# An adaLN block on one core: the attention gate spread by TensorE, one x load on another queue, and a new written-out order

## The chip, the cores and the metric

The kernel runs on one core of a Trainium2 chip. The metric is the device time in microseconds (us) of one execution, given as the median over several executions; lower is better. The core's engines are named as the profile names them: PE (TensorE, with PEld for its weight loads), DVE (VectorE), ACT (ScalarE), POOL (GpSimd) and SP (SyncE, which only issues DMAs here). A q behind a name (SPq, ACTq) stands for an engine's instruction queue when it issues DMAs.

## The reference

x has 2048 rows of 640 values, in bf16. A condition vector c gives six rows of 640, `mod = silu(c) @ w_mod`: shift, scale and gate for the attention (sa, ca, ga) and for the feed-forward part (sb, cb, gb).

```python
h = layernorm(x) * (1 + ca) + sa
x = x + ga * attention(h)      # 32 heads of 20, window of 256 keys, causal
h = layernorm(x) * (1 + cb) + sb
x = x + gb * ((sigmoid(h @ w_gate) * (h @ w_up)) @ w_down)   # 1536 wide
```

Attention is `softmax(q k^T / sqrt(20)) v @ wo`, where a row sees itself and the 255 rows before it.

## The kernel before, in words

The rows are worked in eight chunks of 256 (two blocks of 128). For each chunk the kernel does: statistics and normalisation (DVE and POOL), a transposition of the normalised rows to hT, scaling and shifting, the projection to q, k and v (PE, `proj`), transposition of q and k, attention in two halves of 16 heads, the output projection (`wo`), the second normalisation, and the feed-forward part (`mlpg`, `mlpu`, `down`). Transpositions of chunks 0 to 2 are matmuls against an identity (`aptr`, `qtr`), later ones are DMA transposes on SP's queue (`atr`, `qkt`, `btr`).

A half of attention is five score sets on PE (chunk 0 has three), each followed by its exponentials on ACT (line 1015). All score sets write the one PSUM tile S, so a score set waits for the exponentials of the one before. POOL then masks the exponentials (line 1040). The product with v of one half (`pv`, line 669 with E and V) is issued together with the second score set of the next half, except in chunk 0, where it stands alone. All other products of PE go to four PSUM buffers, the pool M. A `pv` needs two neighbouring buffers of it.

The gates are worked into weights: row-wise products make `wo` into `wo * ga` (line 1253, `wos`, five DVE instructions) and `w_down` into `w_down * gb` (line 1192, `wds`). For that each of the 128 partitions needs the whole gate. `mod_rows` computes it: 20 small matmuls (`modb`) leave the row in four 160-wide strips on four groups of 32 partitions, one DVE instruction (line 710, `gq`) copies the strips to SBUF, and then there are two ways, chosen by the tuple `GB`. With the index in `GB`, TensorE spreads the row (`spread` and `evg`). Otherwise the row goes through DRAM: one small DMA writes it (line 731, `gate`), another reads it back to all partitions (`gatebc`). Both gates use the one buffer `gq` and the one buffer `gbc`. In the kernel before `GB` is empty.

The other half of the PSUM tile of `modb` holds a shift or scale row. It is transposed by DVE (line 736, `modt`) through the tile T1, which attention's normalisation (line 1082) uses too, and the M buffer is held until then.

The order of all 2121 operations is written out. The n-th entry of the list `PRIO` belongs to the n-th operation that the program creates. Its remainder by 5 is the engine (0 PE, 1 ACT, 2 DVE, 3 POOL, 4 SP), and the operations of an engine run in rising order of the entries. A planner in the kernel only picks buffers by estimated times; the waits on the chip come from the data and from buffers that are reused.

At the start ACT's queue issues the load of c, and SP's queue issues x block 0, the first fifth of the scale and shift columns of w_mod (`wm0`, five slices of 320 KB into the space of `wd`), x block 1, the other four slices, then pieces of wqkv. Matmuls without use warm PE meanwhile. The shift and scale (`modA`, tile S, ten matmuls for each slice) end in `mA` (line 761), which hT of chunk 0 needs (lines 846 and 847).

Of the kernel before, what the change touches and what calls it, by code (L numbers as in the profile page):

```python
# [336 lines left out]
def c_pe(n):  # L337
# [5 lines left out]
    23, 28, 258, 8, 43, 33, 958, 18, 1448, 38, 3, 507, 513, 72, 67, 48, 53, 58, 76, 84, 104, 99, 144, 149, 154, 159,  # L343
    164, 344, 169, 334, 329, 174, 584, 734, 739, 754, 604, 759, 749, 764, 594, 120, 177, 181, 192, 197, 62, 105,
    110, 115, 130, 135, 13, 125, 200, 205, 210, 215, 220, 225, 230, 345, 370, 352, 599, 2054, 1659, 1649, 729, 744,
    92, 87, 187, 237, 242, 247, 253, 263, 272, 267, 280, 275, 290, 300, 305, 286, 317, 296, 322, 311, 376, 357, 386,
    367, 362, 412, 422, 391, 417, 396, 380, 400, 406, 620, 655, 672, 515, 521, 820, 827, 465, 470, 476, 530, 535,
    541, 495, 501, 665, 677, 480, 485, 491, 565, 570, 576, 545, 551, 630, 652, 525, 555, 561, 625, 660, 681, 685,
    691, 930, 977, 765, 770, 792, 915, 920, 927, 805, 810, 816, 830, 835, 841, 437, 432, 442, 427, 447, 452, 458,
    463, 642, 647, 890, 845, 775, 900, 710, 897, 852, 797, 907, 787, 980, 985, 996, 1150, 1165, 1171, 1095, 1101,  # L350
    1375, 1382, 1195, 1250, 1257, 1262, 1210, 1296, 1385, 1392, 990, 1105, 1111, 1080, 1085, 1092, 1365, 1371, 1300,
    1351, 940, 945, 951, 971, 1155, 1161, 1190, 1231, 1215, 1220, 1226, 1280, 1285, 1292, 1330, 1337, 1344, 1619,
    1347, 1502, 2249, 1434, 2959, 1669, 1622, 1917, 1932, 2107, 2137, 1395, 1497, 1664, 2754, 1627, 1847, 339, 589,
    1022, 637, 1037, 802, 782, 912, 1043, 1048, 1053, 1058, 1237, 1485, 1410, 1455, 1435, 1305, 1492, 1421, 1462,
    1442, 1317, 1570, 1575, 1581, 1515, 1520, 1527, 1844, 1585, 1590, 1632, 1751, 1839, 1905, 1965, 2041, 2020,
    2030, 2037, 2059, 2070, 2080, 2086, 2142, 2094, 1820, 1830, 1922, 1970, 2075, 2152, 719, 724, 1007, 1002, 1017,
    1012, 937, 1027, 1033, 1063, 1068, 1203, 1242, 1209, 1249, 1453, 1548, 1536, 1543, 1471, 605, 611, 616, 695,
    706, 701, 855, 961, 881, 871, 861, 968, 888, 878, 868, 1115, 1127, 1122, 1137, 1142, 1147, 1736, 1716, 1726,
    1416, 1941, 1070, 1076, 1131, 1175, 1181, 1186, 1265, 1321, 1401, 1356, 1271, 1328, 1408, 1363, 1278, 1505,
    1597, 1512, 1602, 1612, 1772, 1896, 1891, 1886, 1881, 2046, 2310, 2315, 2322, 2155, 2160, 2327, 2205, 2210,  # L360
    2227, 2395, 2400, 2432, 2337, 2332, 2507, 2437, 2502, 2512, 2518, 2523, 2527, 2537, 2534, 2544, 2717, 2756,
    2777, 2772, 2767, 2739, 2734, 2969, 3074, 3022, 3312, 3327, 3027, 3032, 3037, 3317, 3502, 3507, 3322, 3413,
    3418, 2865, 2870, 2875, 2890, 2895, 2760, 2845, 2880, 2885, 2905, 2901, 2912, 3045, 3050, 3075, 3080, 3085,
    2915, 2920, 3055, 3060, 3065, 3091, 3097, 3110, 3115, 3170, 3175, 3180, 3100, 3105, 3185, 3195, 3200, 3191,
    3232, 3205, 3210, 3215, 3220, 3225, 3240, 3245, 3250, 3265, 3270, 3236, 3277, 3280, 3285, 3290, 3295, 3330,
    3300, 3375, 3380, 3385, 3390, 3336, 3422, 3430, 3435, 3445, 3450, 3470, 3440, 3575, 3580, 3585, 3590, 3476,
    3597, 3640, 3645, 3655, 3727, 3650, 3730, 3780, 3817, 3859, 3740, 3745, 3750, 3827, 3900, 3905, 3910, 3917,
    4476, 1700, 1705, 1862, 1710, 1800, 1902, 1914, 1690, 1695, 1746, 1782, 2189, 2390, 2405, 2412, 2145, 2300,
    2307, 2429, 2250, 2260, 2267, 2616, 2749, 1865, 1875, 1937, 1825, 1975, 1992, 1429, 1314, 1607, 1637, 1787,
    1767, 1777, 1792, 1798, 1853, 2008, 2178, 1963, 2128, 2184, 2134, 2367, 2371, 2386, 2381, 2376, 1465, 1481,  # L370
    1476, 1530, 1556, 1566, 1670, 1731, 1676, 1721, 1741, 1805, 1816, 1811, 1870, 1946, 2001, 2025, 2061, 2066,
    1553, 1763, 1758, 1563, 1688, 1683, 1928, 1858, 1953, 1958, 2013, 2018, 2095, 2101, 2231, 2202, 2217, 2222,
    2592, 2597, 2984, 2964, 2999, 2989, 3129, 2255, 2286, 2271, 2341, 2281, 2345, 2351, 2356, 2440, 2456, 2451,
    2465, 2485, 2496, 2460, 2580, 2587, 3399, 2695, 2700, 2817, 2951, 3409, 2620, 2625, 2631, 2445, 2490, 2562,
    3404, 2665, 2670, 2787, 2792, 4199, 2640, 2655, 2662, 2705, 2710, 2841, 1654, 1644, 1997, 1987, 2122, 1982,
    2112, 2117, 2168, 2173, 2193, 2243, 2603, 2608, 2424, 2744, 3346, 3261, 3306, 3041, 3011, 2565, 2576, 2571,
    2238, 2298, 2293, 2198, 2473, 2278, 2363, 2483, 2478, 2548, 2553, 2558, 2635, 2676, 2686, 2652, 2647, 2782,
    2812, 2822, 2974, 2994, 2979, 3004, 3124, 3545, 3550, 3557, 3455, 3540, 3562, 3530, 3535, 3677, 3610, 3615,
    3682, 3572, 3567, 3672, 3687, 3692, 3697, 3703, 3708, 3867, 3712, 3929, 3719, 4213, 4208, 4081, 4132, 4232,
    4220, 4280, 4285, 4290, 4325, 4215, 4310, 4315, 4320, 4335, 4331, 4357, 4345, 4350, 4370, 4375, 4380, 4340,  # L380
    4390, 4395, 4400, 4405, 4386, 4412, 4420, 4425, 4430, 4435, 4440, 4415, 4540, 4545, 4550, 4555, 4511, 4582,
    4560, 4565, 4570, 4585, 4605, 4590, 4595, 4610, 4615, 4620, 4696, 4702, 4705, 4710, 4715, 4725, 4755, 4720,
    4730, 4735, 4800, 4805, 4761, 4812, 4815, 4820, 4825, 4830, 4840, 4835, 4845, 4855, 4860, 4865, 4851, 4872,
    4900, 4905, 4910, 4917, 5215, 5220, 5225, 5382, 5389, 5175, 5180, 5185, 5192, 5360, 5365, 5400, 5407, 5934,
    2690, 2831, 2801, 2826, 2796, 2850, 2856, 2861, 2925, 3016, 3006, 3135, 3141, 3146, 2613, 2838, 2948, 2683,
    2933, 2808, 2938, 3158, 2943, 3133, 3168, 3163, 3350, 3371, 3366, 3357, 3362, 3427, 3512, 3842, 3864, 3849,
    3874, 3854, 4494, 3460, 3486, 3481, 3466, 3491, 3605, 3621, 3631, 3660, 3761, 3666, 3735, 3890, 3896, 4180,
    4185, 4247, 5034, 4105, 4115, 4122, 4177, 5164, 4110, 4160, 4167, 3885, 3970, 4047, 4174, 3995, 4000, 4006,
    4097, 5029, 3980, 3985, 3991, 4135, 4140, 4242, 2724, 2419, 3722, 2727, 3822, 3497, 3807, 3877, 3883, 3948,
    4067, 4052, 4194, 4204, 4793, 4896, 5061, 4978, 5066, 3765, 3771, 3776, 3153, 3523, 3798, 3528, 3518, 3603,  # L390
    3628, 3803, 3638, 3788, 3758, 3793, 3920, 3931, 3936, 3977, 4102, 4127, 4462, 4467, 4484, 4499, 4474, 4489,
    4649, 4920, 4930, 4987, 4925, 4940, 4992, 5015, 5020, 5077, 4935, 5050, 5082, 5002, 4997, 5007, 5092, 5087,
    5097, 5103, 5108, 5122, 5132, 5154, 5159, 5346, 5351, 5323, 5356, 5328, 5475, 5495, 5530, 5535, 5540, 5455,
    5510, 5515, 5520, 5525, 5546, 5567, 5570, 5575, 5580, 5585, 5590, 5550, 5555, 5560, 5600, 5605, 5596, 5612,
    5670, 5675, 5750, 5780, 5785, 5775, 5830, 5835, 5855, 5870, 5891, 5902, 5885, 5905, 5910, 6005, 6010, 5875,
    5880, 5915, 5920, 5925, 6016, 6022, 6050, 6055, 6060, 6065, 6070, 6025, 6030, 6035, 6040, 6045, 6076, 6082,
    6105, 6110, 6115, 6120, 6125, 6130, 6135, 6140, 6145, 6150, 6156, 6172, 6325, 6330, 6335, 6342, 6760, 6820,
    6860, 6867, 6871, 6670, 6775, 6780, 6787, 6825, 6960, 6965, 6972, 6979, 4020, 4031, 4026, 4036, 4041, 4145,
    4151, 4156, 4250, 4256, 4271, 4360, 4446, 4366, 3943, 4298, 4093, 4013, 4238, 4088, 4228, 4268, 4263, 4278,
    4308, 4303, 4450, 4531, 4526, 4517, 4502, 4522, 4627, 4632, 5044, 4659, 4654, 4639, 5059, 4600, 4661, 4686,  # L400
    4681, 4666, 4740, 4746, 4766, 4875, 4881, 4886, 6455, 6485, 6492, 6480, 6520, 6527, 6539, 6500, 6505, 6551,
    6556, 6564, 6515, 6580, 6587, 6375, 6380, 6497, 6594, 6595, 6600, 6606, 6616, 6614, 5230, 5235, 5377, 5410,
    5480, 5486, 3259, 3341, 3957, 3952, 3962, 3812, 3832, 3837, 3968, 4018, 4057, 4062, 4079, 4074, 4783, 4578,
    4772, 4507, 4692, 4960, 4971, 4966, 4458, 4673, 4678, 4538, 4788, 4778, 4753, 4958, 4798, 4948, 4893, 4953,
# [60 lines left out]
KEEP = 3  # L465
# [841 lines left out]
```

## Time and profile before

| | |
|---|---|
| median of 3 runs | 327.32 us (327.22 to 328.8) |
| profiled execution | 326.59 us |
| its span, first to last instruction | 324.9 us |
| PE busy | 316.7 us (97%) |
| DVE, ACT, POOL busy | 211.9, 212.0, 186.5 us |
| granted PE clock | 1.000 |

The span is what the profile's views are measured on; 1.69 us of the execution's time lie around it. Busy times of an engine are the time in which at least one of its instructions is in flight. A timeline row gives the start, the time that the merged group takes, the engine, the line, the operation, output and input tiles with their shape, the count, and in brackets the idle time of the engine before it and what ended that.

### The profile page before, as it was taken

How to read it: one execution, taken by the hardware profiler on the slowest of the kernel's cores; microseconds unless marked ns; L12 is line 12 of the kernel's file. 1: busy time of each engine (PE TensorE's matmuls, PEld its weight loads, DVE VectorE, ACT ScalarE, POOL GpSimd, SP SyncE). 2: the span in 40 equal slices, each digit the busy share in tenths (PEclk: the TensorE clock that was granted, in tenths of full speed). 3: DMA queues.
4: the chain of work that ended last, by engine and by line, in shares of the span. 5: the costliest groups of instructions: out<-in, count | busy, mean ns of one | idle time of the engine just before them, and what ended most of it. 6: DMA issues, size and time to landing. Idle time of an engine off the chain costs nothing.

```text
span 324.9 us, 11597 instructions
## 1 busy us (share of the span) xinstructions
PE 316.7 (97%) x4872; PEld 222.4 (68%) x4873; DVE 211.9 (65%) x424; ACT 212.0 (65%) x316; POOL 186.5 (57%) x276
## 2 busy tenths in 40 slices
PE   6999999989999999999999999999999999999997
PEld 2565544546876568765786467877786788787885
DVE  5687998778688859674477475837463769264332
ACT  1798986788966687787687867786767764011120
POOL 5119769986658694847585939382939681013000
PEclk9999999999999999999999999999999999999999
DMA  7999599989891373824304483340214032202101
GB/s 232 371 306 337 151 259 202 144 174 215 255 159 22 80 107 81 151 57 105 84 23 80 99 115 95 91 71 5 81 40 88 3 78 53 77 20 64 40 2 40
DMA packets 71694, 37.85 MB, mean 117 GB/s; under 512 B 45274, under 2 KB 70362, under 8 KB 71642
## 3 DMA queue, kind: packets, MB, share of 16 engines
q1 hardware_dynamic: 69088, 35.14, 46.3%
q10 hardware_dynamic: 2554, 1.97, 2.4%
q8 instruction: 38, 0.62, 0.7%
q14 instruction: 14, 0.11, 0.1%
HBM read 21.30 MB, written 5.25 MB: 82 GB/s over the span
## 4 chain that ended last, share of the span: by engine, by line
PE 92%; ACT 3%; DMA 2%; issue 1%; SPq 1%; ACTq 0%; DVE 0%
PE M L668 76%; PE S L669 8%; PE M L669 7%; ACT E L1015 2%; DMA wd<-in_w_mod_dram 2%; SPq L570 1%; ACT hT L811 0%; ACTq L570 0%; ACT hT L839 0%; DVE hT L858 0%; ACT hT L846 0%; PE S L668 0%; DVE x L1230 0%
## 5 line engine op out<-in xcount | busy, mean ns | idle before, releaser
L1015 ACT ACTIVATE E<-S 128x512 bf16<-128x512 f32 (+2 forms) x184 | 150.9, 879 | 48.0 <-PE S L669 47.2
L1040 POOL TENSOR_SCALAR_AFFINE_SELECT E<-E 128x512 bf16<-128x512 bf16 (+1 forms) x176 | 141.9, 832 | 69.1 <-ACT E L1015 67.4
L668 PE MATMUL M<-wqkv,hT 128*128 128x480 bf16 (+1 forms) x340 | 74.0, 355 | 0.6 <-ACT hT L846 0.5
L668 PE MATMUL M<-h2T,wu 128*128 128x256 bf16 x480 | 68.1, 273 | 0.0
L668 PE MATMUL M<-h2T,wg 128*128 128x256 bf16 x480 | 67.8, 273 | 0.0
L668 PE MATMUL M<-wd,hh 128*128 128x320 bf16 (+2 forms) x396 | 58.1, 296 | 0.0
L1211 DVE SCALAR_TENSOR_TENSOR hh<-sig,M 128x512 bf16<-128x512 f32 x48 | 32.5, 681 | 38.1 <-ACT sig L1209 25.6
L1209 ACT ACTIVATE sig<-M 128x512 f32<-128x512 f32 x48 | 28.8, 603 | 43.6 <-PE M L668 41.5
L668 PEld LDWEIGHTS M<-h2T,wu 128*128 128x128 bf16 x480 | 45.9, 98 | 7.7 <-issue 0.4
L668 PEld LDWEIGHTS M<-h2T,wg 128*128 128x128 bf16 x480 | 45.6, 98 | 7.2
L668 PEld LDWEIGHTS M<-wqkv,hT 128*128 128x128 bf16 x340 | 30.1, 98 | 27.6 <-DMA wqkv<-in_A_wqkv_dram 1.7
L668 PEld LDWEIGHTS M<-wd,hh 128*128 128x128 bf16 x396 | 36.8, 98 | 14.3 <-DVE hh L1211 0.2
L669 PEld LDWEIGHTS S<-QT,KT 20*64 20x64 bf16 (+1 forms) x1856 | 19.9, 100 | 21.2 <-ACT E L1015 12.0
L1230 DVE TENSOR_TENSOR x<-M,x 128x320 bf16<-128x320 f32 (+2 forms) x33 | 15.6, 476 | 27.2 <-PE M L668 27.1
L669 PE MATMUL S<-QT,KT 20*64 20x256 bf16 (+5 forms) x1856 | 32.1, 228 | 1.1 <-ACT E L1015 1.1
L776 DVE BATCH_NORM_STATS2 st<-x 128x6 f32<-128x320 bf16 x64 | 28.6, 477 | 2.2 <-DMA x<-in_A_x_dram 1.8
L1082 DVE STREAM_TRANSPOSE T<-M 128x512 f32<-128x512 f32 x32 | 21.5, 697 | 9.5 <-PE S L669 8.3
L668 PE MATMUL M<-wo,oT 128*128 128x320 bf16 x160 | 25.4, 300 | 0.0
L669 PE MATMUL M<-E,V 128*32 128x128 bf16 (+1 forms) x960 | 22.8, 246 | 1.0 <-ACT E L1015 0.4
L781 POOL TENSOR_SCALAR st<-st 128x2 f32<-128x2 f32 x16 | 3.7, 233 | 34.8 <-DVE st L778 34.6
L669 PEld LDWEIGHTS M<-E,V 128*32 128x32 bf16 x960 | 19.2, 97 | 5.5 <-issue 3.1
L1091 DVE STREAM_TRANSPOSE On<-Tn 128x1024 bf16<-128x1024 bf16 x16 | 19.8, 1240 | 0.3
(77 smaller groups left out, 238.9 us busy)
## 6 DMA issues: line engine op xcount, KB each, us to landing
x<-in_A_x_dram SPq DMA_DIRECT2D x24, 160.0 KB, 3.4
doc<-On SPq DMA_DIRECT2D x56, 40.0 KB
wd<-in_B_w_down_dram SPq DMA_DIRECT2D x4, 480.0 KB
wd<-in_w_mod_dram SPq DMA_DIRECT2D x5, 320.0 KB
wqkv<-in_A_wqkv_dram SPq DMA_DIRECT2D x4, 400.0 KB
wu<-in_w_mod_dram SPq DMA_DIRECT2D x5, 320.0 KB
out_dram<-x SPq DMA_DIRECT2D x9, 160.0 KB
oT<-doc SPq DMA_DIRECT2D x7, 192.0 KB, 2.8
```

What stands on the lines that cost most here:

```text
L570: return e.dma_start(dst(), src())
L668: return e.matmul(o, l, r, start=st, stop=sp, skip_group_check=True)
L669: return e.matmul(o, l, r, start=st, stop=sp, tile_position=tp, skip_group_check=True)
L776: A("dve", lambda e, g, bi=bi, j=j: e.bn_stats(v(bi * 12 + j * 6, 6), src[bi].ap[:, j * 320:(j + 1) * 320]), 0.48, reads=[src[bi].r()], wr ...
L781: A("pool", lambda e, g: e.tensor_scalar(v(28, n), var(), EPS, None, op0=ALU.add), 0.2, reads=[st.r(("m", bi)) for bi in range(n)], writes ...
L1015: A("act", lambda e, eng: e.activation(dst(), src(), ACT.Exp, scale=SM_SCALE), c_act(n), reads=[Sp.r()], writes=[E.r(key)], prio=3, tag=f" ...
L1040: A("pool", lambda e, eng: e.affine_select(rows(dst), rows(src), pattern=[[0, 8], [sign, n]], compare_op=ALU.is_ge, fill=0.0, base=base, c ...
L1082: A("dve", lambda e, g, h=h: e.transpose(T1.ap[:, 512 * h:512 * h + 512], X[h].ap), 0.694, reads=[X[h].r()], writes=[T1.r(h)], prio=3.5, t ...
L1091: A("dve", lambda e, g: e.transpose(On.ap[:], Tn.ap[:]), 1.22, reads=[Tn.r()], writes=[On.r()], prio=4, tag=f"tr2_{a}")
L1209: A("act", lambda e, g, pg=pg, sg=sg: e.activation(sg.ap[:], pg.ap[:], ACT.Tanh, scale=0.5), c_act(512), reads=[pg.r()], writes=[sg.r()], ...
L1211: A("dve", lambda e, g, pu=pu, sg=sg, f0=f0: e.scalar_tensor_tensor(out=hh.ap[:, f0:f0 + 2, :], in0=sg.ap[:].rearrange("p (a b) -> p a b", ...
L1230: A("dve", lambda e, g, ps=ps, bi=bi, c0=c0, n=n: e.tensor_tensor(x1[bi].ap[:, c0:c0 + n], ps.ap[:, 0:n], x1[bi].ap[:, c0:c0 + n], op=ALU. ...
```

## The change

Four edits, with the list replaced by one of 2123 entries:

```diff
-GB = ()
+GB = (1,)
...
     def load_x(pool, b, prio, tmin=0.0, eng="sp", extra=()):
...
-            tag=f"x{b}" ..., eng=eng, lat=0.6 if b < 2 else 0.2 + DSAFE, extra=extra)
+            tag=f"x{b}" ..., eng=eng, lat=(0.6, 0.9)[b] if b < 2 else 0.2 + DSAFE, extra=extra)
...
-    keep[0], keep[1] = load_x(p_x1, 0, 0), load_x(p_x1, 1, 0, tmin=1.2)
+    keep[0], keep[1] = load_x(p_x1, 0, 0), load_x(p_x1, 1, 0, eng="act", tmin=1.25)
```

`tmin` and `lat` are figures for the planner alone. With `GB = (1,)` the first of the two `mod_rows`, the attention's gate, takes the branch that was there unused. For each half of the row two matmuls with a broadcast column of the identity as weights copy a strip to all partitions (`gbm`), and one instruction moves 128x320 values from PSUM to `gbc` (`gbe`):

```python
for half in range(2):
    pb = Tile(p_M, "gb")
    def spread(e, g, half=half, pb=pb):
        for j in (2 * half, 2 * half + 1):
            ins = mm(e, pb.ap[:, j % 2 * 160:j % 2 * 160 + 160], ident[:, 32 * j:32 * j + 1].to_broadcast([128, 128]), gq[:],
                     j % 2 == 0, True)
        return ins
    ...
    def evg(e, g, half=half, pb=pb):
        ...
        return e.activation(dst, src, ACT.Copy) if g == "act" else e.tensor_copy(dst, src)
```

The feed-forward gate still goes through DRAM. The new list puts the first `gbe` on DVE and the second on ACT. Read out by engine around the gate, the two lists give (operation and its running number; hyphen: before, plus: after):

```diff
 PE
-aptr2#4 modb#0 qtr1#4 qtr1#1 qtr1#3 modb#1 aptr2#1 aptr2#3 aptr2#2 score1#0 aptr2#0 pvs0#1 projq2#2 projq2#3 score1#1 projq2#0 projq2#1 projk2#0 projk2#1 score1#2
+aptr2#4 qtr1#5 modb#0 qtr1#4 aptr2#1 aptr2#3 gbm#0 qtr1#1 qtr1#3 score1#0 modb#1 aptr2#2 gbm#1 aptr2#0 pvs0#1 projq2#2 score1#1 projq2#3 projk2#0 projq2#0 projq2#1 score1#2
 DVE
-ahTe2#4 gq#0 modt#0 evqt1#1 evqt1#3 ahTe2#3 ahTe2#2 ahTe2#0 gq#1 modt#1 tr1_0#3 evqk2#1 tr1_0#2
+ahTe2#4 evqt1#5 gq#0 modt#0 ahTe2#3 gbe#0 evqt1#1 evqt1#3 ahTe2#2 gq#1 wos#0 modt#1 amodu3#3 tr1_0#3 astats4#0 tr1_0#2
 ACT
-exp0#13 n_ow_0#3 ahTe2#1 amodu3#4 exp1#1 exp1#0 amodu3#2 exp1#2
+exp0#13 ahTe2#1 exp1#1 gbe#1 ahTe2#0 exp1#0 n_ow_0#3 amodu3#1 exp1#2
 SP, start
-x0 wm0#0 x1 wm0#1 wm0#2 wm0#3 wm0#4 wq wk x3 x2 wk x4 wq wv x5
+x0 wm0#0 wm0#1 wm0#2 wm0#3 wm0#4 wk wq x2 x3 wk wq x5 x4 wv
 SP, feed-forward gate
-btr0 btr0 x12 wd wd atr5 qkt3 gatebc#1 wu1
+btr0 btr0 wd gate#1 x13 wu1 wd gatebc#1 atr5 qkt3
```

`ahTe2` moves a transposed block of chunk 2 from PSUM to hT with scale and shift, `tr1_0` reads the product `pvs0` out of PSUM, `evq..` are moves out of PSUM. Elsewhere some 75 operations change their engine between ACT, DVE and POOL or their place by a few; among them four of the five scalings of h2T of chunk 0 (`bmodu0`) go from DVE to POOL. Up to the score sets and products of attention that close each stage, PE has the same operations to do in both lists, but for a few that cross such a mark and for the two new `gbm`.

More of the change, by code (lines that the diff above doesn't have):

```diff
@@ L597, in load_x @@
         dma(lambda: t.ap[:], lambda: x_flat[b * 128:(b + 1) * 128, :], 0.5, writes=[t.r()], prio=prio, tmin=tmin,
-            tag=f"x{b}" if pool is p_x0 or b < 2 * KEEP else f"y{b}", eng=eng, lat=0.6 if b < 2 else 0.2 + DSAFE, extra=extra)
+            tag=f"x{b}" if pool is p_x0 or b < 2 * KEEP else f"y{b}", eng=eng, lat=(0.6, 0.9)[b] if b < 2 else 0.2 + DSAFE, extra=extra)
         return t
```

234 rows, old and new, of the table PRIO are left out of this document.

## The prediction

> **What bounds the kernel now.** I read the head of the page first, then the busy times by stage, the waits of PE, and the timeline where PE waits.
>
> ```profile
> span 324.9 us, 11597 instructions
> PE 316.7 (97%) x4872; PEld 222.4 (68%) x4873; DVE 211.9 (65%) x424; ACT 212.0 (65%) x316; POOL 186.5 (57%) x276
> ```
>
> Busy times by stage (stretch in us, its length, then PE, PEld, DVE, ACT, POOL, each with its count):
>
> ```profile
> 38.00:76.00 38.00, 35.76 (x631) 18.67 (x632) 32.13 (x68) 30.06 (x44) 31.06 (x46) 1.00 0.97 204
> 76.00:322.50 246.50, 246.43 (x3850) 183.86 (x3850) 151.26 (x285) 155.03 (x223) 137.13 (x185) 1.00 0.37 78
> ```
>
> From 76 us on PE is busy 246.43 of 246.50 us: three quarters of the kernel are a queue of matmuls, and an order that leaves the matmuls as they are can move nothing there, up or down, unless it makes a wait that is not there now. PE stands still for 8.2 us in all (324.9 - 316.7): 2.24 (38.00 - 35.76) between 38 and 76, some 2.5 behind the last matmul, where the last sums are stored, and the remaining 3.5 before 38 us. So the middle and the start, the first 76 us, are where this change can win or lose.
>
> PE's own waits in 38 to 60 and in 60 to 72 us:
>
> ```profile
> PE M L669 <- DVE hT L858: 0.3, 1, 0.3
> PE S L669 <- ACT E L1015: 0.2, 1, 0.2
> ...
> PE S L669 <- ACT E L1015: 0.9, 3, 0.4
> PE M L669 <- ACT E L1015: 0.4, 1, 0.4
> ```
>
> So what PE waits for in the middle is mostly ACT's exponentials; the list shows no wait for the attention's gate.
>
> **The start: x block 1 on ACT's queue.** SP's issues of x block 1 and of the four slices behind it, then the share of the DMA engines (next to last column) with GB/s behind it, then PE's wait for a slice:
>
> ```profile
> 1.71 0.42 SPq L570 DMA_DIRECT2D x<-in_A_x_dram  x1
> 2.18 1.86 SPq L570 DMA_DIRECT2D wd<-in_w_mod_dram  x4
> ```
>
> ```profile
> 2.00:3.00 1.00, 1.00 (x4) 0.31 (x3) 0.03 (x1) 0.68 (x1) 1.00 (x8) 1.00 0.96 262
> 7.00:8.00 1.00, 0.00 (x0) 0.00 (x0) 0.43 (x2) 0.00 (x0) 0.53 (x1) 1.00 1.02 367
> ```
>
> ```profile
> 8.25 0.47 PE L668 MATMUL S<-silubc,wd 128*128 128x64 bf16 x10 [1.61 <-DMA wd<-in_w_mod_dram]
> ```
>
> Without x in between, the last four slices of wm0 are issued 2.18 - 1.71 = 0.47 us earlier. If issuing sets their arrival, the first projection comes 0.47 us earlier. If the transfers set it, nothing comes earlier, because x block 1 still has to be moved, at the same time. The DMA engines are full (0.96 in the third microsecond, 1.02 in the eighth), while SP is done with the slices at 4.04 (2.18 + 1.86) and PE waits for one until 8.25. That is the picture of transfers that set it. I take a gain of 0.1, with 0.47 as one end and a loss of 0.3 as the other (x block 1 arriving late, or the pieces of wqkv in their new order wk, wq). The Trainium skill (DMA: Bandwidth & Descriptors, section Issuing engines are not separate DMA queues) speaks against the edit in the same way: DMAs of all queues run on the same 16 engines and interleave, and a second queue saves only the time to issue. By that rule the term is 0, by the issue times alone it is -0.47; the full DMA engines of the rows agree with the rule.
>
> **The gate's way through DRAM, taken out.** It goes `gq`, then two DMAs on SP, then `wos`:
>
> ```profile
> 36.40 0.68 SPq L569 DMA_DIRECT2D gate<-gq  x1
> 38.24 0.33 SPq L570 DMA_DIRECT2D gbc<-gate  x1
> 43.81 0.48 DVE L1253 TENSOR_TENSOR wo<-wo,gbc 128x640 bf16<-128x640 bf16 x1
> 58.28 1.52 PE L668 MATMUL M<-wo,oT 128*128 128x320 bf16 x10
> ```
>
> The first `wos` stands in its place in DVE's order 5.2 us after the read was issued (43.81 - 38.57), without idle time before it, and `wo` is used at 58.28. Taking the DMAs out saves SP's queue 1.01 us (0.68 + 0.33), so that the loads behind them are issued a little earlier, and PE nothing: 0. If that cover were gone it would be worth the two flights; it is 14 us long (58.28 - 43.81). The new `wos` at the front of DVE's queue gains nothing either, for the same reason.
>
> **The gate's way through PE, put in.** Four 160-wide matmuls. Nearest rows are one of 320 and one of 128 width:
>
> ```profile
> 296.12 6.68 PE L668 MATMUL M<-wd,hh 128*128 128x320 bf16 x48
> 35.93 0.84 PE L668 MATMUL M<-ident,stg 128*128 128x128 bf16 x12
> 45.99 0.47 ACT L893 ACTIVATE stg<-M 128x320 bf16<-128x320 f32 x1
> 33.65 0.49 DVE L894 CAST stg<-M 128x320 bf16<-128x320 f32 x1
> ```
>
> 6.68/48 = 0.14 and 0.84/12 = 0.07 us each; the width is nearer to 128, so 4 x 0.07 = 0.28 us of PE (0.28 to 0.56). The two evictions are 0.49 us on DVE and 0.47 us on ACT. They go in front of other work, and this is where the cost lies. The rows of the stage before, PE, DVE and ACT:
>
> ```profile
> 35.13 0.86 PE L669 MATMUL M<-wu,silubc 128*32 128x320 bf16 x20
> 38.15 0.43 PE L669 MATMUL S<-QT,KT 20*64 20x256 bf16 x24
> 39.15 0.84 PE L669 MATMUL M<-E,V 128*32 128x256 bf16 x32 [0.35 <-DVE hT L858]
> 41.04 0.43 PE L669 MATMUL S<-QT,KT 20*64 20x256 bf16 x24
> ```
>
> ```profile
> 36.05 0.33 DVE L710 TENSOR_SCALAR gq<-M 128x160 bf16<-128x160 f32 x1
> 37.19 0.68 DVE L894 CAST KT<-M 128x512 bf16<-128x512 f32 x1
> 44.21 0.34 DVE L736 STREAM_TRANSPOSE T<-M 128x160 f32<-128x160 f32 x1
> ```
>
> ```profile
> 37.89 0.56 ACT L857 ACTIVATE hT<-M,mA 128x256 bf16<-128x256 f32 x1 [0.45 <-PE M L668]
> 38.85 1.92 ACT L1015 ACTIVATE E<-S 128x1536 bf16<-128x1536 f32 x2
> 47.59 1.45 ACT L1015 ACTIVATE E<-S 128x1536 bf16<-128x1536 f32 x1 [0.94 <-PE S L669]
> ```
>
> I follow the new order by hand. `modb#0` ends at 36.0 (35.13 + 0.86) as now. PE then has eight small matmuls (0.5 us) and stands before `gbm#0` at 36.5. That needs `gq#0`, which DVE does behind a 512-wide move that was ACT's (0.68): not at 36.05 but about 36.5, ended 36.8. So PE waits some 0.4 us that it does not wait now. With `gbm#0` (0.14), eight transposes (0.5) and the score set (0.36) PE is at about 37.9. ACT begins the 1.45 us exponential at about 38.1, ends 39.55, does `gbe#1` to 40.0 and the last move to hT (0.56) to 40.55. Meanwhile PE does `modb#1`, two transposes and `gbm#1` (0.86 as for `modb#0`, and 0.4) and stands before the product with v (`pvs0#1`) at 39.2. It needs two neighbouring buffers of the four of M. All four hold results: `modb#1` (until its transpose, now 44.21, later in the new order), two blocks for hT and `gbm#1`. The pair comes free at 40.0 at the earliest (`gbe#1`) and at 40.55 at the latest. Now the product starts at 39.15. PE has done the same operations by then, and the two `gbm`: it is behind by 0.9 to 1.4 us, its own 0.28 included.
>
> Queued behind the waiting product are the score set (41.04 now) and chunk 2's projections, and ACT's exponentials wait for that score set. Part of the delay is taken up again, because score sets wait for ACT now. The idle time of the weight loads before them, in 38 to 60 us:
>
> ```profile
> PEld S L669 <- ACT E L1015: 1.5, 3, 0.6
> PEld S L669 <- ACT V L893: 0.4, 1, 0.4
> PEld S L669 <- ACT stg L893: 0.4, 1, 0.4
> PEld S L669 <- issue: 0.2, 1, 0.2
> ```
>
> That is 2.3 us at five score sets. A set that waited for nothing but the issue shows 0.2 of it, so some 1.3 us (2.3 - 5 x 0.2) is the most that can be taken up, and about half of that where ACT is late itself, which it is here by `gbe#1`. Of a lag of 1.2, the middle, 0.6 is left (between 0 and all of 1.4).
>
> **The rest.** Four scalings of h2T of chunk 0 go from DVE to POOL:
>
> ```profile
> L812 POOL TENSOR_SCALAR h2T<-h2T,scB,shB x19: 551/554/1113, 114.8 to 299.3; 128x256 bf16<-128x256 bf16 x19
> 75.37 0.33 DVE L812 TENSOR_SCALAR h2T<-h2T,scB,shB 128x256 bf16<-128x256 bf16 x1
> 77.97 0.27 PE L668 MATMUL M<-h2T,wu 128*128 128x256 bf16 x1
> ```
>
> 4 x 0.55 = 2.2 us from 75.4 ends at 77.6, before the first matmul that needs it (77.97 now, behind one more score set in the new order): 0, and up to 0.5 if POOL is busy with masks. The feed-forward gate's write moves behind the first load of `w_down`, and SP has to wait there until it has landed, but reads it back before two DMA transposes, not behind them: 0. Its reader waits so long for it now:
>
> ```profile
> DVE wd L1192 <- DMA gbc<-gate: 0.4, 1, 0.4
> ```
>
> That wait may go or grow off PE's path. Near the end the order of PE differs by a few places within matmuls that need no new input: 0.
>
> **Sum.** Start -0.1, waits and `gbm` +0.6, the rest 0: +0.5 us. The profiled execution took 326.59 us (span 324.9), 0.73 below the median; 326.59 + 0.5 = 327.1 for it, and 327.32 + 0.5 = 327.8 us for the median. The three runs spread by 0.5%, so 0.5% (1.6 us: 325.7 to 329.0) is what I call no change.
>
> **The rivals.**
> *The buffers stay short (slower).* The lag is not taken up: `modb#1` holds its buffer beyond 47 us, because its transpose comes behind attention's transposes of T1, and the moves of chunk 2's q out of M come later in DVE's order too; two more chains then wait for a buffer, each for most of a 512-wide move (0.68). 1.4 + 2 x 0.5 = +2.4, 329.7 us; ACT, whose exponentials alternate with the score sets, carries it on. It decides from the point where the product with v starts later than about 40.6. For it: all four buffers are taken at that place. Against it: the stage after has score sets that wait for ACT anyway.
> *The middle gets better (faster).* The list is new everywhere in the first 76 us, and the 2.24 us of PE's idle time in 38 to 76 may go, with the 0.47 of the start: -2.7, 324.6 us. For it: those waits are of ACT's order, which the list sets. Against it: between the two products with v of chunk 1 both lists give PE the same operations, and ACT the same four scalings among the exponentials.
> *It does nothing.* The lag is taken up wholly, and `gbm` lies in idle time: 327.2 us, the start's 0.1 below now.
>
> **How the numbers follow.** The forecast 0.38 (0 to +1.6 us: 327.3 to 329.0), doing nothing or a little better 0.17 (down to 325.7), buffers short 0.26, the middle better 0.19. Faster by over 0.5% is the last, 0.19; slower the third, 0.26; within 0.5% the first two, 0.55. The range 325.2 to 329.9 leaves out about half of each outer case, 0.1 below and 0.1 above.
>
> **What would show it.** Right: no DMA to `gbc` near 38 us; the first projection within 0.3 us of where it is; idle time of PE before `gbm#0` and the product with v at 39 to 41 us, the latter released by a move of ACT; from 76 us to the end the same 246.4 us of PE. Wrong: PE idle after 76 us, a slice of wm0 landing 0.4 us earlier, or less than 1.5 us of idle time in 38 to 76.

## The result, and the profile after

The changed kernel takes 328.52 us in the median, the kernel before 327.26 us beside it (22 executions each, 326.7 to 330.9 and 326.2 to 328.8). The ratio is 1.0043, 95% interval 1.0028 to 1.0059: slower by 0.4%, within the half per cent that the prediction calls no change, and the interval does not hold 1. In six of the 22 executions the mean granted clock is 0.995 instead of 1.000, and these take 329.8 to 330.9 us; the median of the other sixteen is 328.11. The profiled execution took 328.01 us (before: 326.59), its span is 326.3 us (before: 324.9).

Head of the page of the changed kernel, then its busy times by stage (stretch, its length, PE, PEld, DVE, ACT, POOL with counts, granted clock, share of the DMA engines, GB/s):

```profile
span 326.3 us, 11588 instructions
...
PE 317.7 (97%) x4876; PEld 222.8 (68%) x4877; DVE 207.4 (64%) x420; ACT 214.2 (66%) x318; POOL 186.6 (57%) x280
```

```profile
38.00:76.00 38.00, 34.65 (x589) 18.09 (x582) 30.25 (x68) 28.20 (x40) 29.91 (x44) 1.00 0.83 205
76.00:324.00 248.00, 247.71 (x3887) 184.35 (x3885) 148.17 (x280) 158.38 (x228) 137.57 (x189) 1.00 0.36 79
```

The long queue of matmuls is as it was: 0.29 us of idle time (248.00 - 247.71) after 76 us, 0.07 before. The loss lies in the middle: PE stands for 3.35 us (38.00 - 34.65) between 38 and 76, where it stood for 2.24.

What PE waits for in the changed kernel (in all, how often, longest), and the places in its timeline:

```profile
PE S L669 <- ACT E L1015: 1.7, 3, 1.2
...
PE M L669 <- ACT gbc L726: 0.7, 1, 0.7
```

```profile
7.50 0.46 PE L668 MATMUL S<-silubc,wd 128*128 128x64 bf16 x10
...
10.61 0.43 PE L668 MATMUL M<-wqkv,hT 128*128 128x320 bf16 x2 [0.51 <-DVE hT L847]
```

```profile
38.59 0.30 PE L668 MATMUL M<-gq,ident 128*128 128x160 bf16 x2
39.73 0.84 PE L669 MATMUL M<-E,V 128*32 128x256 bf16 x32 [0.73 <-ACT gbc L726]
51.82 0.43 PE L669 MATMUL S<-QT,KT 20*64 20x256 bf16 x24 [1.22 <-ACT E L1015]
57.44 1.50 PE L669 MATMUL M<-E,V 128*32 128x128 bf16 x64
```

The third slice of wm0 is used at 7.50 instead of 8.25, the first projection starts at 10.61 instead of 11.22. Then two waits that are longer than in the kernel before: 0.73 us before the product with v at 39.73 (0.35 before), released by the eviction of the gate on ACT, and 1.22 us before a score set at 51.82 (0.17 before the same set at 49.59). ACT's timeline shows where both come from (a q behind ACT: issues of DMAs), with a line of DVE's below:

```profile
37.85 1.45 ACT L1015 ACTIVATE E<-S 128x1536 bf16<-128x1536 f32 x1 [0.20 <-PE S L669]
...
39.20 0.43 ACT L726 ACTIVATE gbc<-M 128x320 bf16<-128x320 f32 x1
...
46.02 3.70 ACTq L570 DMA_DIRECT2D doc<-On  x6
49.83 1.94 ACT L1015 ACTIVATE E<-S 128x512 bf16<-128x512 f32 x2 [3.36 <-DMA doc<-On]
```

```profile
44.76 1.23 DVE L1091 STREAM_TRANSPOSE On<-Tn 128x1024 bf16<-128x1024 bf16 x1
```

The first is the one that the prediction follows by hand. The second was not in it: the new list puts six writes of attention's result (`doc<-On`) in one row into ACT's order, in front of two exponentials. The row starts when DVE's transposition has made the result (45.99, first issue at 46.02), issuing takes 3.70 us, and ACT computes nothing for 3.36 us of that. In the kernel before, two of the six are issued earlier and the other four behind these two exponentials, and ACT issues them while the exponentials run (47.59 to 49.53):

```profile
47.66 1.65 ACTq L570 DMA_DIRECT2D doc<-On  x3
48.94 0.59 ACT L1015 ACTIVATE E<-S 128x512 bf16<-128x512 f32 x1
49.35 0.35 ACTq L570 DMA_DIRECT2D doc<-On  x1
```

The starts of the products with v are the marks by which the runs below are compared. Up to each mark PE has the same work in all kernels but for the `gbm`. Starts in us, from the timeline of PE, and the last addition of the kernel, from that of DVE:

| kernel | 1st | 2nd | 3rd | 4th | 5th | last addition |
|---|---|---|---|---|---|---|
| before | 28.32 | 39.15 | 56.07 | 71.62 | 89.51 | 322.49 |
| after | 27.83 | 39.73 | 57.44 | 72.90 | 90.75 | 324.01 |
| difference | -0.49 | +0.58 | +1.37 | +1.28 | +1.24 | +1.52 |

So 0.49 us are won at the start, 1.07 lost before the second mark, 0.79 before the third, and of the rest 0.15. These are single executions: in the four kernels below that have x block 1 on ACT's queue and the old order, the first mark lies anywhere from 27.19 to 28.13.

### The profile page after: what moved, and what is told of

Read it like the earlier page. It is cut to its first block, busy times and chain, and to the rows that moved or that the text cites. A ratio compares the mean times of both kernels' runs of the same rounds, so it can differ in the third digit from the quotient of the medians.

```text
span 326.3 us, 11588 instructions
## 1 busy us (share of the span) xinstructions
PE 317.7 (97%) x4876; PEld 222.8 (68%) x4877; DVE 207.4 (64%) x420; ACT 214.2 (66%) x318; POOL 186.6 (57%) x280
## 4 chain that ended last, share of the span: by engine, by line
PE 76%; issue 0%; ACT 0%; DVE 0%
PE M L668 64%; PE S L669 6%; PE M L669 6%; ACT E L1015 0%; DVE x L1230 0%
## 5 line engine op out<-in xcount | busy, mean ns | idle before, releaser
L668 PE MATMUL M<-wqkv,hT 128*128 128x480 bf16 (+1 forms) x340 | 73.1, 355 | 1.5 <-DVE st L776 0.6
L668 PE MATMUL M<-h2T,wg 128*128 128x256 bf16 x480 | 67.0, 273 | 0.0
L668 PEld LDWEIGHTS M<-h2T,wg 128*128 128x128 bf16 x480 | 46.4, 98 | 6.8
L668 PEld LDWEIGHTS M<-h2T,wu 128*128 128x128 bf16 x480 | 44.9, 98 | 7.7 <-issue 0.2
L894 DVE CAST stg<-M 128x480 bf16<-128x480 f32 (+1 forms) x29 | 16.6, 577 | 7.2 <-PE M L668 6.9
```

Of the source, the lines that this page charges most:

```text
L668: return e.matmul(o, l, r, start=st, stop=sp, skip_group_check=True)
L894: return e.tensor_copy(dst(), src())
```

## The experiments

All times are medians of executions beside the kernel before on the same chip, which took 326.8 to 327.2 us there. Operations are named as in the lists above; `n_ow_0` are the writes to `doc`, `exp1` the exponentials of chunk 1, `glu_0` the products of the gated unit of chunk 0.

### Only x block 1 on ACT's queue

```diff
 kernel before, SP, start
-x0 wm0#0 x1 wm0#1 wm0#2 wm0#3 wm0#4
+x0 wm0#0 wm0#1 wm0#2 wm0#3 wm0#4
 ACT, start
-c cth
+c x1 cth
```

> The kernel before with x block 1 issued by ACT's queue behind c, nothing else changed. Issue time sets the arrival (theory A): third and fourth slice of wm0 land 0.4 to 0.7 us earlier (their matmuls at 7.5 and 8.3 instead of 8.25 and 9.01), first projection at 10.6 to 10.8 instead of 11.22, last matmul 0.4 to 0.6 earlier, 326.7 us. The transfers set it (theory B, the forecast's): slices and first projection within 0.15 us of the kernel before, 327.2 us. The rest of the new order makes the early start, such as wk before wq (theory C): as B.

Measured: 326.38 us, ratio 0.9988 (0.9968 to 1.0009). The timeline of PE at the start, then of SP, DVE and PE later on:

```profile
7.02 0.47 PE L668 MATMUL S<-silubc,wd 128*128 128x64 bf16 x10
...
10.37 1.87 PE L668 MATMUL M<-wqkv,hT 128*128 128x320 bf16 x12 [0.47 <-ACT hT L846]
```

```profile
74.79 4.29 SPq L803 DMA_TRANSPOSE KT<-stg  x1
79.13 0.58 SPq L570 DMA_DIRECT2D gbc<-gate  x1
```

```profile
84.29 2.60 DVE L1192 TENSOR_TENSOR wd<-wd,gbc 128x640 bf16<-128x640 bf16 x4 [2.73 <-DMA gbc<-gate]
```

```profile
87.64 1.25 PE L668 MATMUL M<-h2T,wu 128*128 128x256 bf16 x10 [1.08 <-DVE hh L1211]
```

The third slice is used 1.23 us earlier than before (7.02 against 8.25), the first projection 0.85 earlier. In this execution that is more than the 0.47 us that x's issue took from SP. The marks show where the gain goes: -1.13, -1.13, -0.63, -0.62, and then +0.62 at the fifth. Half a microsecond of it goes before the third mark, where PE waits 0.73 us (0.22 before). Between the fourth and the fifth mark a transposing load of K holds SP's queue for 4.29 us (3.19 before), the read of the feed-forward gate behind it is issued at 79.13 (77.77 before), DVE stands for 2.73 us (0.37 before) in front of a scaling of `wd` that PE needs from 98.62 on, and PE waits 1.08 us for the product behind that. This execution took 327.20 us. Seven of the twelve took 325.45 to 326.40, less than each of the 17 executions of the kernel before beside them (326.63 to 328.50); in those the gain may have been kept, but none of them was profiled, and the interval of the ratio holds 1.

### x block 1 on SP's queue, behind all five slices

```diff
 kernel before, SP, start
-x0 wm0#0 x1 wm0#1 wm0#2 wm0#3 wm0#4
+x0 wm0#0 wm0#1 wm0#2 wm0#3 wm0#4 x1
```

> The kernel before with x block 1 still on SP's queue, but issued behind the five slices of wm0. If what counts is that the slices are issued earlier or have fewer bytes ahead of them, they land 0.4 to 0.7 us earlier as in e1_x1_act, and x block 1 lands 1 to 2 us later, so that its normalisation (DVE, 7.57 to 8.37 in the kernel before) ends near 9.5 and the gain is lost again at the transposes: 327.0 to 327.6 us. If the second queue itself counts, the slices land as in the kernel before.

Measured: 331.46 us, ratio 1.0142 (1.0124 to 1.016).

```profile
PE M L668 <- DVE x L796: 4.0, 1, 4.0
```

```profile
8.42 0.47 PE L668 MATMUL S<-silubc,wd 128*128 128x64 bf16 x10
12.88 0.98 PE L668 MATMUL M<-ident,x 128*128 128x128 bf16 x8 [3.99 <-DVE x L796]
```

The fourth slice is there by 8.42 instead of 9.01, so order of issue does order arrival; but x block 1 itself comes too late, and PE waits 3.99 us for its normalised rows; then the granted clock is 0.50 for 3.4 us. The expectation had the block 1 to 2 us later and a time of 327.0 to 327.6 us, which is missed. The use of ACT's queue is that neither stands behind the other.

### Only the gate through TensorE, in the old order

```diff
 kernel before
-GB = ()
+GB = (1,)
 PE
-modb#0 qtr1#4 qtr1#1 qtr1#3 modb#1 aptr2#1
+modb#0 qtr1#4 qtr1#1 qtr1#3 gbm#0 modb#1 gbm#1 aptr2#1
 DVE
-evqt1#3 ahTe2#3
+evqt1#3 gbe#0 ahTe2#3
 ACT
-exp1#1
+gbe#1 exp1#1
```

> The kernel before with attention's gate alone taken through TensorE, in the old order (two gate products on PE, one eviction on DVE, one on ACT; the second block of x stays on SP, the six doc writes stay split). If the gate's price is its own instructions: 0.28 us of PE and nothing else, products with v at 28.3, 39.2 to 39.5, 56.4, end +0.3, so 327.2 to 327.6 us. If it is the M buffers that the gate products hold (the forecast's lag), the second product with v comes 0.9 to 1.4 later than 39.15 and the end is 0.6 to 1.4 later: 327.6 to 328.4 us.

Measured: 328.02 us, ratio 1.0028 (1.001 to 1.0046). Busy times between the first and the second mark and between the second and the third (stretch, length, PE and so on as above), first of the kernel before, then of this one:

```profile
28.32:39.15 10.83, 10.48 (x179) 6.13 (x179) 9.23 (x18) 10.08 (x19) 8.26 (x13) 1.00 0.67 201
39.15:56.07 16.92, 16.52 (x226) 7.86 (x226) 15.24 (x35) 13.48 (x20) 13.66 (x20) 1.00 1.07 239
```

```profile
28.61:40.29 11.68, 11.04 (x182) 6.39 (x183) 9.68 (x19) 10.46 (x20) 9.12 (x15) 1.00 0.64 185
40.29:56.92 16.63, 16.45 (x226) 7.84 (x226) 14.88 (x33) 13.44 (x19) 12.53 (x18) 1.00 0.88 224
```

The way from the first to the second mark is 0.85 us longer: 0.56 in PE's busy time (11.04 - 10.48), which is what the four `gbm` take, and 0.29 in idle time (0.64 instead of 0.35). The way to the third mark is 0.29 us shorter, 16.63 us instead of 16.92: 0.22 in idle time (0.18 instead of 0.40) and 0.07 in PE's busy time. So the standing is taken up again, the matmuls' own time is not, and 0.56 us are left at the third and at the fourth mark. At the last addition it is 1.14 us, counted from the first mark, and 0.87 by the medians; what adds the rest is not followed here.

### Both named edits, in the old order

The two edits of the first and the third experiment together, nothing else.

> The kernel before with both named edits (second block of x on ACT's queue, attention's gate through TensorE), in the old order. If the two add up (0.6 earlier for the one, 0.9 later for the other): 327.1 to 327.8 us, first product with v near 27.3, second 38.9 to 39.2, third 56.0; what the changed kernel takes beyond that, 0.7 to 1.4 us, is the new order's. If the edits work against each other beyond the sum, 328.2 to 328.8 us as the changed kernel, and the new order costs nothing.

Measured: 326.73 us, ratio 0.9987 (0.9971 to 1.0002).

```profile
39.10 0.84 PE L669 MATMUL M<-E,V 128*32 128x256 bf16 x32 [0.16 <-POOL hT L812]
49.53 0.43 PE L669 MATMUL S<-QT,KT 20*64 20x256 bf16 x24 [0.17 <-ACT E L1015]
```

The first mark is at 27.42 (-0.90), the second is 11.68 us behind it (+0.85, as with the gate alone), the third at 55.73, the fourth at 71.41, the last addition at 322.52 (+0.03). The score set that waits 1.22 us in the changed kernel waits 0.17 here. By the time the two edits add up to nothing that shows (327.1 to 327.8 us were expected), and the interval lies wholly below that of the changed kernel (1.0028 to 1.0059): what the changed kernel loses, some 1.4 us by the medians (+1.26 against -0.09), comes with the new list. Counted from the first mark of each, the changed kernel is behind this one by 0.22 at the second, 1.30 at the third, 1.08 at the fourth mark and 1.08 at the last addition: that loss arises between the second and the third mark, where the row of writes is.

### The row of six writes, put into the old order

```diff
 kernel before, ACT (moves left out; exponentials run together)
-exp1 n_ow_0#1 exp1 n_ow_0 exp1 n_ow_0 exp1 exp1#9 exp1#8 n_ow_0 x4
+exp1 n_ow_0#1 exp1 x3 n_ow_0 x6 exp1#9 exp1#8
```

> The kernel before with the six doc writes in one row on ACT's order, as the changed kernel has them, and nothing else. If the row holds ACT and with it the score sets: a wait of ACT of 3 to 4.6 us for doc near 46 to 50, PE idle 1 to 2.5 us behind it, third product 57 to 58.5, the time 328.3 to 330 us. If the row is harmless in itself and only the new order makes it cost: within 0.4 of 327.0 us.

Measured: 330.99 us, ratio 1.0119 (1.0089 to 1.015). Timeline of ACT, timeline of PE, and busy times by stage right behind:

```profile
48.62 3.60 ACTq L570 DMA_DIRECT2D doc<-On  x6
52.32 1.94 ACT L1015 ACTIVATE E<-S 128x1536 bf16<-128x1536 f32 x2 [3.93 <-DVE wo L1253]
```

```profile
54.31 0.65 PE L669 MATMUL S<-QT,KT 20*64 20x256 bf16 x24 [3.17 <-ACT E L1015]
```

```profile
54.00:55.00 1.00, 0.69 (x25) 0.51 (x26) 0.00 (x0) 0.26 (x1) 1.00 (x2) 0.66 1.16 177
55.00:56.00 1.00, 1.00 (x3) 0.33 (x3) 0.00 (x0) 0.95 (x2) 0.93 (x2) 0.50 1.03 341
56.00:57.00 1.00, 1.00 (x4) 0.43 (x3) 0.68 (x2) 0.99 (x1) 0.90 (x3) 0.50 0.35 100
```

The row by itself holds ACT for 3.93 us, PE for 3.17 us, and then PE's clock falls to 0.50 for 3.4 us (54.3 to 57.7). (The profile names a product of DVE as what ended ACT's idle time; the issues fill it.) The issues are slow, not waiting for data: DVE's transposition has ended at 48.59, the first issue starts at 48.62, and they follow each other at 0.60 us each (3.60/6). From the second to the third mark this kernel takes 21.23 us (62.11 - 40.88), the kernel before 16.92: of the 4.31 us between them 2.77 are more idle time of PE (3.17 instead of 0.40), and 1.54 are PE's longer busy time (18.06 instead of 16.52), part of it at half the clock. This part of the new list is harmful in the old surroundings, more than in the new ones. This execution took 332.81 us, 1.82 above the median; its first mark is 1.73 us late (30.05), since the clock fell once more at the start, which is not the row's.

### The row of six writes taken out of the changed kernel, two ways

Once behind the next pair of exponentials in one row, once split as in the kernel before. The second way also puts the second read of what was written (`oT_0#1`) behind two more exponentials.

```diff
 changed kernel, ACT, first way
-n_ow_0 x6 exp1#8 exp1#9
+exp1#8 exp1#9 n_ow_0 x6
 second way (moves left out)
-exp1 exp1 exp1 exp1 n_ow_0 x6 exp1#8 exp1#9 exp1 exp1 oT_0#0 oT_0#1 exp1#12 exp1#13
+exp1 n_ow_0 exp1 n_ow_0 exp1 exp1 exp1#8 exp1#9 n_ow_0 x4 exp1 exp1 oT_0#0 exp1#12 exp1#13 oT_0#1
```

> The changed kernel with the six writes of attention's output of chunk 0 moved on ACT's queue from in front of the exponentials of the third set of chunk 1's first half (exp1#8) to behind the second of them (exp1#9). Theory D (those writes hold ACT and so PE): ACT's 3.36 us of idle time and PE's 1.22 us before the score set at 51.8 go, the product with v now at 57.44 comes at 56.1 to 56.5, and the end is 0.9 to 1.3 us earlier: 327.3 us. Theory E (the forecast's: the lag at the product at 39.73 is what is carried on): the product stays at 57.0 or later and the end moves by less than 0.4 us.

> The changed kernel with the six doc writes split over ACT's order as the kernel before has them (two between the edge exponentials, four further back), and the read of their output behind them. If the row of six writes on ACT costs the changed kernel its third and fourth product: ACT's wait of 3.4 us is gone, PE's 1.2 us near 51 too, third product 56.0 to 56.6 (changed kernel 57.44), the end 0.8 to 1.3 earlier: 327.2 to 327.7 us. If the lag at 39.7 is what carries to the end, the wait moves to another place and the time stays at 328.2 to 328.8 us.

First way, measured: 329.14 us, ratio 1.0071 (1.0055 to 1.0087). Timelines of ACT and of PE:

```profile
53.94 1.40 ACTq L570 DMA_DIRECT2D oT<-doc  x2
55.44 1.94 ACT L1015 ACTIVATE E<-S 128x512 bf16<-128x512 f32 x2 [2.70 <-PE M L668]
```

```profile
57.48 1.50 PE L669 MATMUL M<-E,V 128*32 128x128 bf16 x64 [1.50 <-ACT E L1015]
```

The 1.22 us before the score set are gone, but the two reads of what was written (`oT<-doc`) stand in ACT's order too, now hold the exponentials behind them, and PE waits 1.50 us one stage later. The wait was moved, with some added.

Second way, measured: 328.34 us, ratio 1.0035 (1.0015 to 1.0056).

```profile
58.09 0.43 PE L669 MATMUL S<-QT,KT 20*64 20x256 bf16 x24
59.58 1.52 PE L668 MATMUL M<-wo,oT 128*128 128x320 bf16 x10 [1.07 <-DVE T L1082]
```

ACT's long wait is gone, and the third mark comes 28.30 us after the first (56.65 - 28.35), where the changed kernel takes 29.61: 1.31 us better, and equal to the 28.31 of the gate alone. From the second to the third mark PE is busy for all of the 16.44 us; in the changed kernel it is busy for 16.49 of 17.71, and the 1.22 us between are the wait for the row. Then PE stands for 1.07 us before the output projection, and of the gain 0.23 is left at the fourth mark (44.84 after the first, the changed kernel 45.07); the times of the two are not told apart. The profile puts that wait down to DVE's transposition, of which the later half ended at 59.93 (58.62 + 1.31), after PE had begun; in the changed kernel the same product started (59.23) before that transposition did (59.41), and by the kernel's own choice of buffers the product needs none that the transposition reads. What it needs last is the read `oT_0#1`. Its issue started at 54.35 (changed kernel 53.14), its last packet ended at 58.82 and the product started 0.76 us later; in the changed kernel these are 58.35 and 0.88, without a wait, in the first way 59.18 and 0.89. So the wait comes from the read, which this experiment moved as well; the writes split with the read left in its place were not run.

### The gate back through DRAM in the new order

```diff
 changed kernel
-GB = (1,)
+GB = ()
 (gbm, gbe left out; SP: gate#0 behind the second x, gatebc#0 behind two wu; wos#0 on DVE behind divide)
```

> The changed kernel with the attention gate through DRAM again (write behind the loads of x8, read in front of x11, the first scaling of wo where the kernel before had it), all else in the new order. Theory E (the gate's matmuls and evictions cost, and the cost is carried on): the product with v now at 39.73 comes at 39.0 to 39.3, and the end is 0.5 to 0.9 us earlier: 327.7 us. Theory D: the product comes earlier too, but the six doc writes still end when DVE's On lets them, the wait before 51.8 grows by most of it, and the end moves by less than 0.4 us: 328.2 us.

Measured: 330.67 us, ratio 1.0114 (1.0092 to 1.0135).

```profile
39.58 0.84 PE L669 MATMUL M<-E,V 128*32 128x256 bf16 x32 [1.04 <-DVE hT L812]
52.91 0.65 PE L669 MATMUL S<-QT,KT 20*64 20x256 bf16 x24 [2.36 <-ACT E L1015]
```

```profile
46.28 4.54 ACTq L570 DMA_DIRECT2D doc<-On  x6
```

```profile
53.00:54.00 1.00, 1.00 (x26) 0.56 (x27) 0.00 (x0) 0.35 (x1) 1.00 (x1) 0.50 1.29 273
```

Without `gbm` and `gbe` the second mark still is 11.98 us behind the first (39.58 - 27.60; changed kernel 11.90, before 10.83). In the new list the lag is there without the gate. The profile puts PE's wait down to a scaling of hT on DVE, which this product does not need. It needs a buffer of M that the move of the last block to hT frees; in the new list that move stands on ACT behind the long exponential, and it ends at 39.44. So it is the order, and it does not add to the gate's lag. The row of six writes takes 4.54 us here, PE stands for 2.36, and its clock falls to 0.50 behind that, for 3.4 us. Both expectations for the time (327.7 and 328.2 us) are missed.

### Two attempts to keep what x on ACT's queue wins

```diff
 kernel before, x1 on ACT, SP (first attempt)
-btr0 btr0 x12 wd wd atr5 qkt3 gatebc#1
+btr0 btr0 gatebc#1 x12 wd wd atr5 qkt3
 kernel before, x1 on ACT, DVE (second attempt)
-glu_0#0 wds x4 glu_0#1 glu_0#2 glu_0#3 wds x4
+glu_0#0 glu_0#1 wds x3 glu_0#2 glu_0#3 wds x5
```

> The kernel before with the second block of x on ACT's queue and the feed-forward gate's read put on SP's queue ahead of the transposing loads that held it up to 79.1 in the run with x alone. If that late read is what gave the 0.6 to 1.1 us back: no wait of DVE for the gate near 84, the fifth product with v at 88.4 to 88.9 (before 89.51), the end 0.6 to 1.1 earlier, 325.9 to 326.4 us. If the gain is lost to something else late (hidden in the middle's other waits), the DVE wait is gone and the end stays at 326.8 to 327.3 us. If the read ahead pushes the transposing loads of K later, the third or fourth product is late by what the read costs on the queue.

> The kernel before with the second block of x on ACT's queue, and three of the first four products of the down weights with the gate (DVE) put behind the next product of the gated unit, the fourth two further back. If the 0.6 to 1.1 us that x on ACT's queue won were lost only because DVE stood 2.7 us before those products, waiting for the gate's read: PE's wait of 1.1 us for hh is gone, the fifth product with v at 88.4 to 89.0, the end 0.6 to 1.1 earlier than the kernel before, 325.9 to 326.5 us. If other waits between 72 and 90 take it anyway: 326.7 to 327.4 us.

First attempt, measured: 328.09 us, ratio 1.0032 (1.0004 to 1.006). DVE no longer waits for the gate, but the load of x that now is issued behind the gate's read is late. Timeline of DVE, of PE, and a stretch of the stages:

```profile
77.14 0.49 DVE L776 BATCH_NORM_STATS2 st<-x 128x6 f32<-128x320 bf16 x1 [1.24 <-DMA x<-in_A_x_dram]
77.55 2.27 DVE L812 TENSOR_SCALAR h2T<-h2T,scB,shB 128x256 bf16<-128x256 bf16 x3
```

```profile
79.87 0.39 PE L668 MATMUL M<-h2T,wu 128*128 128x256 bf16 x2 [1.33 <-DVE h2T L812]
```

```profile
82.00:84.00 2.00, 2.00 (x11) 1.42 (x10) 1.06 (x1) 1.03 (x2) 1.31 (x3) 0.50 1.07 352
```

The statistics of that block stand on DVE ahead of three scalings of h2T, PE waits 1.33 us for them, and in this execution the clock fell to 0.50 after it. It took 330.44 us, well above the median.

Second attempt, measured: 326.66 us, ratio 0.9993 (0.9975 to 1.0011). The wait of 1.08 us for hh is gone, but the three scalings of `wd` now take 3.06 us where the four took 2.60, and the product behind them is late for the fifth mark:

```profile
85.23 3.06 DVE L1192 TENSOR_TENSOR wd<-wd,gbc 128x640 bf16<-128x640 bf16 x3
```

```profile
89.63 1.50 PE L669 MATMUL M<-E,V 128*32 128x128 bf16 x64 [0.53 <-DVE hh L1211]
```

The start of this execution won 0.26 us at the first mark (28.06), and the fifth is at 89.63, 0.12 later than before. Neither attempt makes a kernel that is shown to beat the one before.

## Why the prediction was right, point by point

The time (328.52 us, forecast 327.8, range 325.2 to 329.9) and the case (within 0.5%) came out as said. The sum came near with the gate's lag right, the start too small, and the row of writes missing.

- **The start, -0.1 (from -0.47 to +0.3): mis-sized.** At the first mark it is -0.49. In the eight profiled executions with x block 1 on ACT's queue the first projection starts at 10.35 to 11.24, at 10.74 in the mean, against 11.22 in the kernel before: -0.48. The other two with x on SP's queue in its old place start at 11.15 (the gate alone) and at 13.23 (the row of writes, where the clock fell meanwhile). So the end "if issuing sets their arrival" is the nearer one in the mean; single executions lie between no gain and 0.87, and the size is known no better than that. The step that failed is "That is the picture of transfers that set it": full DMA engines show that something is being moved, not whose turn it is. By the rule in the Trainium skill (DMA: Bandwidth & Descriptors, section Issuing engines are not separate DMA queues) a second queue saves the time to issue, and the mean of -0.48 against 0.47 agrees with that; that this be nothing, as the prediction read it, does not. The list named "a slice of wm0 landing 0.4 earlier" and a first projection off by over 0.3 us as signs of error, and both were there.
- **The gate's way through DRAM, taken out: 0.** Nothing contradicts it: no wait of the kernel before lies there, and none appeared. The cover of 14 us is counted from the first of the five scalings; the last one ends at 56.55, 1.7 us before `wo` is used.
- **The gate's way through PE, lag of 0.9 to 1.4 us at the product with v: right in place, releaser and size; its parts were not.** +1.07 us, released by `gbe#1` on ACT behind the exponential of 1.45 us (begun at 37.85; `gbe#1` from 39.20 to 39.63), product at 39.73. The matmuls themselves were taken at 4 x 0.07 = 0.28 us, "the width is nearer to 128"; with the gate alone they make 0.56, the other end of that term, 0.14 each. The wait of 0.4 us before `gbm#0` did not come; the profile shows none there. And the gate is not the only cause: alone it makes 0.85 in the old order, and the new order makes 1.15 (11.98 - 10.83) without it.
- **"Half taken up", 0.6 left: right in amount for the gate, not for the kernel.** With the gate alone 0.56 us are left at the third mark, all of it PE's own work, and the waits are taken up wholly. With the writes split in the new list PE has no idle time left between the second and the third mark, so there they are taken up too; in the changed kernel the row's wait of 1.22 us takes their place.
- **"The rest: 0": this is what is missing.** The prediction goes through four moved scalings and the feed-forward gate's write. The six writes that the new list puts together in ACT's order, and the reads behind them, are not in it, though the two lists have them in different places. They make the wait of 1.22 us between the second and the third mark (+0.79 in all there), and with the writes split again the third mark is 1.31 better. A wait further on takes most of that, for the read that was moved with them; so that the time of the new list without the row, and with nothing else moved, stays open. The step that failed is where ACT's order is compared: the sentence on "the same four scalings among the exponentials" looks only at the stretch between the two products with v of chunk 1 (third to fourth mark, where it holds: +1.37 to +1.28), and at computing alone, while DMA issues are work of ACT's queue as well. The four scalings of h2T on POOL and the write moved past the load of `w_down` cost nothing that shows: from the third mark to the fifth the difference goes from +1.37 to +1.24.
- **From 76 us on the same 246.4 us: nearly.** 0.29 us of idle time instead of 0.07, and +0.28 from the fifth mark to the last addition.
- **The rivals.** "The buffers stay short" was to decide from a product later than 40.6; it started at 39.73, and the waits that came later are of ACT's row of writes, not of buffers of M; what it gave, 329.7, is 1.2 above. "The middle gets better" is refuted: 3.35 us of idle time instead of less than 2.24. "It does nothing" holds, by the time, for the two edits without the new list (0.9987), and not for the change as made.

So -0.49 + 1.07 + 0.79 + 0.15 = +1.52 us in the profiled executions against a forecast of +0.5: the terms that were left out and undersized have opposite signs, and a part of them cancelled. That the time fell 0.7 us from the forecast is partly luck.

## What to carry to other kernels

Where an order is written out, list what a queue issues together with what its engine computes: a row of six small writes on ACT cost more than the gate's whole way through TensorE, and moving the row only moved the wait to the reads behind it. Issues that stand behind an exponential run beside it; a row of them in front of one holds it up. A gain at the start can be lost where another queue orders the work, here SP with its transposing loads; follow it from mark to mark, in more than one execution, before it is counted. And a large reordering that comes with small edits is best taken apart by making the edits in the old order: here they cost nothing that shows, and the new order was the loss.

## What the runs showed of the hardware

- **Issues on ACT's queue.** A write of 40 KB to DRAM takes ACT 0.28 to 0.98 us to issue in the changed kernel, 3.70 us for six, 4.54 us for six without the gate's products, while the DMA engines are full (share 1.03 to 1.20 in each of the microseconds from 46 to 50 of the changed kernel); in these rows ACT computes nothing meanwhile. Exponentials that ACT has already begun go on beside issues: in the kernel before four issues from 47.66 to 49.70 lie beside two exponentials from 47.59 to 49.53. The issue of one transposing load of K on SP's queue took 1.51, 3.19 and 4.29 us in three kernels. What sets these times no run here separates.
- **The clock after a short stand.** After waits of PE of 2.36, 3.17 and 3.99 us the granted clock fell to 0.50, each time for 3.4 us, and in two executions so after shorter ones: after 1.33 us (the gate's read put early), and at the start of the kernel with the row in the old order after 0.55 and 1.03 us. After 1.22 us in the changed kernel, 1.50 us in the first way of moving the writes and 1.61 us in the kernel before it stayed at 1.00. The Trainium skill (TensorE: Matmul & The Clock Gate, section What's actually happening) has the clock fall after about 3.4 us of an idle window; most of the falls here came after less, and not after every stand of the same length. As an estimate from these numbers, 3.4 us at half speed make a mean clock of 0.995 over 330 us, so that each of the six slower executions of the changed kernel had one such fall; where, was not profiled.
- **The same product on DVE.** A scaling of 128x640 (`wd<-wd,gbc`) took 0.42 us in the mean of five (2.08/5) and 1.02 in the mean of three (3.06/3), with the same tiles in the second attempt's kernel; POOL masked exponentials beside the slow ones (85.15 to 88.81) and stood idle beside most of the fast ones (until 91.18). That the one makes the other is not shown.
